# Tile 0's feed-forward products and pair 2's transposes: whole TensorE columns or halves of them

## The chip, the cores and the metric

The kernel runs on one core of one Trainium2 chip. The metric is the device time of one execution in microseconds; lower is better. TensorE (PE) does the matrix products, with its weight loads listed apart as PEld; VectorE (DVE), ScalarE (ACT), GpSimd (POOL) and SyncE (SP) do the rest. The DMA queues on POOL, SP and ACT carry the transfers.

## The reference

A retention layer is followed by a gated feed-forward layer. For 4 batches, 8 heads, 768 tokens and a head size of 64:

```
state = gamma[h] * state + k[t] (outer) v[t]      # for each batch and head
y[t]  = (1 / sqrt(64)) * q[t] @ state
x     = y as (3072 tokens, 512)
out   = (sigmoid(x @ w_gate) * (x @ w_val)) @ w_out     # w_gate, w_val: 512 x 1536; w_out: 1536 x 512
```

All inputs are float32; the kernel computes its products in bfloat16 and accumulates in float32.

## The kernel before

The 768 tokens of each batch are cut into 6 tiles of 128 tokens. A tile takes all 4 batches, so it is 512 rows of the feed-forward layer. The retention part of a tile is done in two *pairs* of batches: pair i belongs to tile i // 2 (pairs 0 and 1 to tile 0, pair 2 and 3 to tile 1, and so on).

For each pair, the keys and queries are needed with the head size on the partitions (`kqT`). Pairs 0 and 1 get this by transposes on TensorE (`first_transpose`), pair 2 by `transpose(2, j)`, which multiplies with an identity matrix, and the pairs from 3 on by DMA transposes (`xbar`, tile `kqX`). Then come the scores (`scores` for tile 0, `quarter_scores` later, L248), their masking on VectorE (`mask`), the part of y that comes from the state (`inter`, L271), the part within the tile (`intra`, L278), the copy of y into `xT` (`y_out`), and the state itself (`first_state` for tile 0, L378; `state`, L301).

For each tile, the feed-forward layer is done in 12 groups, one for each slice n1 of 128 hidden columns: a gate product and a value product over 4 slices kk of the model size, a sigmoid on ScalarE and a multiplication on VectorE into `hT`. Then `down` does the output products, four blocks b of 128 rows, each a sum over the 12 slices, with a copy on ScalarE and a store.

The schedule is written by hand: the order of the calls is the order of the instructions on each engine. A `plan` says after which feed-forward group a retention step of a later tile is inserted. PSUM has 8 banks in rotation (`bank`); an instruction that takes a bank waits until its last reader is done.

Tile 0 has an order of its own. Its first four hidden slices are computed by `first_parts` (L409), which takes the products as the weights and the columns of x arrive; slices 4 and 5 by `up_part`; then `first_state` for both pairs; then slices 6 to 11; then `down` for tile 0, with the transposes, scores, y and state of pair 2 between its parts.

How a product is issued is the matter of the change. `product(split, o, w, x)` issues either one matmul with 128 weight columns (which the profile lists as 128*128), or two with 64 weight columns each, whose results go to the lower and the upper 64 partitions (128*64). It is line L391 for both. In tiles 1 to 5 the products are in halves; in tile 0 they are whole, apart from the last six of block 3. `first_parts` calls the matmul itself, always whole. The two retention products `intra` and `state` are in halves anyway (a head has 64 columns), and `quarter_scores` and `inter` use quarters of the array (64*64).

`transpose` does whole transposes, for two heads at once: each takes 128 columns of k or q, and fills 128 partitions of the bank.

Of the kernel before, what the change touches and what calls it, by code (L numbers as in the profile page):

```python
# [15 lines left out]
def kernel(  # L16
# [12 lines left out]
    nc = tc.nc  # L29
    B, H, S, D = q.shape  # L30
    N_TOK, D_MODEL = out.shape
    D_FF = moe_w_gate.shape[1]
    C = 128
    NT = S // C
    NP = H // 2
    KT = D_MODEL // 128
    NFF = D_FF // 128
# [14 lines left out]
    def half(e):  # L52
        return slice(e * D, (e + 1) * D)
# [24 lines left out]
    wo = wpool.tile([128, NFF, D_MODEL], BF16, name="wo")  # L78
# [51 lines left out]
    ident = const.tile([128, 128], BF16, name="ident")  # L130
# [69 lines left out]
    def bank(shape, dt=F32):  # L200
        return pf.tile(shape, dt, tag="ff", name="ff")

    def heads(t, j, p):
        return t[:, j * H + 2 * p:j * H + 2 * p + 2, :].rearrange("s h d -> s (h d)")
# [4 lines left out]
    def transpose(i, j):  # L209
        tp = bank([128, 2, NP, C], BF16)  # L210
        for which, x in enumerate((kn[i], qn[i])):
            for p in range(NP):
                nc.tensor.transpose(tp[:, which, p, :], heads(x, j, p), ident)  # L213
        nc.scalar.copy(kqT[i][:, :, j], tp)

    def xbar(i):
# [68 lines left out]
    def x_of(t, kk, lo=0, hi=512):  # L285
        per = NP // len(xT[t])
        return xT[t][kk // per][:, kk % per, lo:hi]
# [20 lines left out]
    def state_sum(i):  # L308
        new_za(i)
        nc.vector.tensor_tensor(za[i], za[i - 2], zz[i], op=ALU.add)  # L310

    def casts(i):
        zb[i] = at.tile([128, 2, NP, D], BF16, tag="zb", name="zb", bufs=4)
        nc.vector.tensor_tensor(zb[i], za[i], tabz[:, i // 2 + 1].unsqueeze(3).to_broadcast([128, 2, NP, D]), op=ALU.mult)  # L314
# [69 lines left out]

    hT = {}

    def product(split, o, w, x, **marks):

        for g in range(2) if split else (None,):
            c = slice(0, 128) if g is None else half(g)  # L390
            nc.tensor.matmul(o[c], w[:, c], x, **marks)  # L391

    def up_part(t, w, n1s, lo=0, hi=512):
        n = hi - lo
        u = bank([128, 512])
        for i, n1 in enumerate(n1s):
            for kk in range(KT):
                product(t > 0, u[:, i * n:(i + 1) * n], w[:, kk, n1 * 128:(n1 + 1) * 128], x_of(t, kk, lo, hi),
                        start=(kk == 0), stop=(kk == KT - 1))
        return u[:, :len(n1s) * n]  # L400

    def first_parts(w, n1s, cut=512):

        us = [bank([128, 512]) for _ in range(2)]
        for k0, lo, hi in ((0, 0, cut), (0, cut, 512), (2, 0, 512)):
            for n1, u in zip(n1s, us):
                for kk in range(k0, k0 + 2):
                    if lo < hi:
                        nc.tensor.matmul(u[:, lo:hi], w[:, kk, n1 * 128:(n1 + 1) * 128], x_of(0, kk, lo, hi),  # L409
                                         start=(lo == 0 and kk == 0), stop=(kk == KT - 1), skip_group_check=True)  # L410
        return us

    def gate_times_val(t, n1s, lo, hi, ps):
# [9 lines left out]
    def up(t, n1s, lo=0, hi=512):  # L423
        gate_times_val(t, n1s, lo, hi, [up_part(t, w, n1s, lo, hi) for w in (wg, wv)])
# [3 lines left out]
    def rows(t, b):  # L428
        return b * S + t * C

    def down(t, b, lo, hi, split=None):
        split = t > 0 if split is None else split
        if lo == 0:
            po[b] = bank([128, 512])
        o = po[b]
        for n1 in range(lo, hi):
            product(split, o, hT[t][:, n1, b * C:(b + 1) * C], wo[:, n1, :], start=(n1 == 0), stop=(n1 == NFF - 1))
        if hi < NFF:
            return
        ob = ffn.tile([128, D_MODEL], F32, tag="ob", name="ob", bufs=4)  # L440
        nc.scalar.copy(ob, o)  # L441
        nc.sync.dma_start(out=out[rows(t, b):rows(t, b) + C, :], in_=ob)

    def last_down(t):
        row = rows(t, B - 1)
        lo = 0
        for i, width in enumerate((256, 128, 128)):
            o = bank([128, 512])
            for n1 in range(NFF):
                product(True, o[:, :width], hT[t][:, n1, 384:512], wo[:, n1, lo:lo + width],  # L450
                        start=(n1 == 0), stop=(n1 == NFF - 1))

            for g in range(1 + i // 2):
                n = width // (1 + i // 2)
                ob = ffn.tile([128, n], F32, tag=f"ob{i}{g}", name="ob", bufs=1)
                copy, eng = (nc.vector.tensor_copy, nc.sync) if i == 0 or g == 1 else (nc.scalar.copy, nc.scalar)
                copy(ob, o[:, g * n:(g + 1) * n])  # L457
                eng.dma_start(out=out[row:row + C, lo:lo + n], in_=ob)  # L458
                lo += n
# [47 lines left out]
    for n1s in ((0, 1), (2, 3)):  # L507
        gates = first_parts(wg, n1s, 3 * C if n1s[0] == 0 else 512)
        for n1, *ps in zip(n1s, gates, first_parts(wv, n1s)):
            gate_times_val(0, (n1,), 0, 512, ps)  # L510
    last_constants()
    zero_scores()
    later_tables()
    gates = [up_part(0, wg, (n1,)) for n1 in (4, 5)]
    for n1, gate in zip((4, 5), gates):
        gate_times_val(0, (n1,), 0, 512, (gate, up_part(0, wv, (n1,))))
# [23 lines left out]
    scale_k(2)  # L540
    new_kqT(2)
    down(0, 0, 0, 6)
    transpose(2, 0)
    down(0, 1, 0, 6)
    transpose(2, 1)
    down(0, 2, 0, 6)
    for b in range(3):
        down(0, b, 6, 9)
# [17 lines left out]
        y_out(2, j)  # L566
    state(2)
    state_sum(2)
    down(0, 3, 6, 12, True)
    casts(2)  # L570


# [12 lines left out]
    for t in range(1, NT):  # L585
        groups = [lambda n1=n1: up(t, (n1,)) for n1 in range(NFF)]
        if t == 1:
            groups = [lambda lo=lo, n1=n1: up(1, (n1, n1 + 1), lo, lo + 256) for lo in (0, 256) for n1 in range(0, NFF, 2)]
        groups += [lambda b=b, lo=lo: down(t, b, lo, lo + 6) for b in range(B) for lo in (0, 6)]
        if t == NT - 1:  # L590
            groups[-2:] = [lambda: last_down(t)]
        for i, group in enumerate(groups):
            group()
            for at_group, step, *g in plan[t]:
                if at_group == i:
                    step(*g)
# [30 lines left out]
```

## Time and profile before

| what | value |
|---|---|
| median of 4 runs | 224.52 us (223.89 to 225.24) |
| the profiled execution: time | 224.95 us |
| the profiled execution: span of the core | 223.2 us |
| granted TensorE clock, mean | 0.998 |
| TensorE busy (matmuls) | 216.3 us, 2760 instructions |
| TensorE busy (weight loads) | 126.4 us, 2760 instructions |
| VectorE, ScalarE, GpSimd busy | 124.8, 70.7, 100.3 us |

The profiled execution's time holds its span and 1.75 us around it. Matmuls overlap in the pipeline, so the time that one takes in a stream is read from the distance between starts and not from the mean duration of a group. A form such as 128*64 128x512 means 128 rows and 64 columns of weights, and 512 columns streamed.

### The profile page before, as it was taken

How to read it: one execution, taken by the hardware profiler on the slowest of the kernel's cores; microseconds unless marked ns; L12 is line 12 of the kernel's file. 1: busy time of each engine (PE TensorE's matmuls, PEld its weight loads, DVE VectorE, ACT ScalarE, POOL GpSimd, SP SyncE). 2: the span in 40 equal slices, each digit the busy share in tenths (PEclk: the TensorE clock that was granted, in tenths of full speed). 3: DMA queues.
4: the chain of work that ended last, by engine and by line, in shares of the span. 5: the costliest groups of instructions: out<-in, count | busy, mean ns of one | idle time of the engine just before them, and what ended most of it. 6: DMA issues, size and time to landing. Idle time of an engine off the chain costs nothing.

```text
span 223.2 us, 6371 instructions
## 1 busy us (share of the span) xinstructions
PE 216.3 (97%) x2760; PEld 126.4 (57%) x2760; DVE 124.8 (56%) x252; ACT 70.7 (32%) x123; POOL 100.3 (45%) x120
## 2 busy tenths in 40 slices
PE   7789999999999999999999999999999999999994
PEld 2543444559999565556556556555555555555554
DVE  6783983094984785656916645925644922333301
ACT  5883232334233213332222332321332322333221
POOL 7999646877796638709568091460000000000000
PEclk9999999999999999999999999999999999999999
DMA  9999999999999999989999999899600012100022
GB/s 132 139 161 183 197 203 172 174 131 248 162 127 148 151 163 146 169 96 62 131 126 184 165 64 106 80 137 140 141 3 0 3 47 97 47 4 1 3 94 94
DMA packets 105964, 25.84 MB, mean 116 GB/s; under 512 B 95056, under 2 KB 102992, under 8 KB 105936
## 3 DMA queue, kind: packets, MB, share of 16 engines
q0 software_dynamic: 80960, 13.90, 82.8%
q1 hardware_dynamic: 23648, 11.18, 24.1%
q10 hardware_dynamic: 1328, 0.36, 0.7%
q8 instruction: 21, 0.34, 0.6%
q14 instruction: 7, 0.06, 0.1%
HBM read 28.31 MB, written 6.29 MB: 155 GB/s over the span
## 4 chain that ended last, share of the span: by engine, by line
PE 90%; POOL 5%; DMA 2%; issue 0%; ACT 0%; ACTq 0%; DVE 0%; POOLq 0%
PE ff L391 81%; PE ff L278 3%; DMA wv<-in_moe_w_val_dram 2%; PE ff L409 2%; PE ff L248 2%; POOL vs L95 2%; PE ff L271 2%; POOL qn L95 1%; POOL kn L95 1%; PE ff L301 1%; POOL wg L82 1%; PE ff L213 0%; PE ff L378 0%; ACT ob L457 0%; ACTq L458 0%
## 5 line engine op out<-in xcount | busy, mean ns | idle before, releaser
L420 DVE TENSOR_TENSOR hT<-gs,ff 128x512 bf16<-128x512 f32 x72 | 48.4, 686 | 50.7 <-PE ff L391 46.8
L391 PE MATMUL ff<-xT,wg 128*64 128x512 bf16 (+2 forms) x608 | 70.1, 346 | 0.0
L391 PE MATMUL ff<-xT,wv 128*64 128x512 bf16 (+2 forms) x608 | 70.0, 345 | 0.0
L419 ACT ACTIVATE gs<-ff 128x512 f32<-128x512 f32 x72 | 42.8, 597 | 84.0 <-PE ff L391 78.6
L391 PE MATMUL ff<-wo,hT 128*64 128x512 bf16 (+3 forms) x582 | 64.7, 361 | 0.0
L391 PEld LDWEIGHTS <-wv 128*64 128x64 bf16 (+1 forms) x608 | 35.4, 109 | 23.5
L391 PEld LDWEIGHTS <-hT 128*64 128x64 bf16 (+1 forms) x582 | 32.7, 109 | 27.1
L391 PEld LDWEIGHTS <-wg 128*64 128x64 bf16 (+1 forms) x608 | 34.7, 109 | 23.1 <-DVE xT L294 0.6
L261 DVE TENSOR_TENSOR st<-ff,maskk 128x256 bf16<-128x256 f32 (+2 forms) x76 | 35.1, 493 | 7.4 <-PE ff L248 6.4
L441 ACT COPY ob<-ff 128x512 f32<-128x512 f32 x23 | 13.5, 586 | 56.5 <-PE ff L391 56.4
L294 DVE TENSOR_TENSOR xT<-ff,taby 128x512 bf16<-128x512 f32 x20 | 12.9, 686 | 23.5 <-PE ff L278 23.5
L224 POOL TENSOR_TENSOR ks<-kn,tabsk 128x1024 bf16<-128x1024 bf16 x8 | 15.4, 1929 | 2.4 <-DMA kn<-in_k_dram 2.2
L537 POOL COPY held<-kqX 128x1 bf16<-128x1 bf16 x7 | 1.3, 187 | 33.5 <-DMA kqX<-qn 31.0
L70 POOL DMA_DIRECT2D kn<-in_k_dram x20 | 15.1, 765 | 2.4 <-DMA kn<-in_k_dram 1.3
L70 POOL DMA_DIRECT2D qn<-in_q_dram x20 | 15.3, 790 | 0.8 <-DMA wv<-in_moe_w_val_dram 0.6
L60 POOL DMA_DIRECT2D vs<-in_v_dram x10 | 12.0, 1205 | 1.7 <-DMA wo<-in_moe_w_out_dram 1.0
L66 POOL DMA_DIRECT2D kn<-in_k_dram x10 | 9.2, 921 | 2.1 <-issue 1.5
L66 POOL DMA_DIRECT2D qn<-in_q_dram x10 | 9.1, 913 | 0.9 <-DMA wv<-in_moe_w_val_dram 0.9
L314 DVE TENSOR_TENSOR zb<-za,tabz 128x512 bf16<-128x512 f32 x10 | 7.3, 735 | 0.0
L464 PE MATMUL ff<-zero 128*128 128x512 bf16 x14 | 5.8, 543 | 1.2 <-DVE zero L139 1.2
L278 PE MATMUL ff<-st,vs 128*64 128x128 bf16 x160 | 6.4, 222 | 0.0
L82 POOL DMA_DIRECT2D wv<-in_moe_w_val_dram x8 | 6.2, 795 | 0.0
(74 smaller groups left out, 114.9 us busy)
## 6 DMA issues: line engine op xcount, KB each, us to landing
out_dram<-ob SPq DMA_DIRECT2D x23, 256.0 KB, 2.6
vs<-in_v_dram POOLq DMA_DIRECT2D x10, 256.0 KB, 7.2
kn<-in_k_dram POOLq DMA_DIRECT2D x13, 128.0 KB, 4.5
qn<-in_q_dram POOLq DMA_DIRECT2D x13, 128.0 KB, 4.8
wo<-in_moe_w_out_dram POOLq DMA_DIRECT2D x4, 384.0 KB, 9.6
kn<-in_k_dram POOLq DMA_DIRECT2D x20, 64.0 KB, 4.6
qn<-in_q_dram POOLq DMA_DIRECT2D x20, 64.0 KB, 4.8
wg<-in_moe_w_gate_dram POOLq DMA_DIRECT2D x4, 256.0 KB, 7.3
```

The source lines that it names most:

```text
L60: nc.gpsimd.dma_start(out=vs[i], in_=v[2 * h:2 * h + 2, :, t * C:(t + 1) * C, :].rearrange("b h s d -> s (b h) d"))
L66: nc.gpsimd.dma_start(out=tiles[i][:, 0:H], in_=src[0])
L70: nc.gpsimd.dma_start(out=dst[:, e], in_=pairs[:, 1 - e])
L95: eng.dma_start(out=dst, in_=x[b:b + n, :, 0:C, :].rearrange("b h s d -> s (b h) d"))
L224: nc.gpsimd.tensor_tensor(ks[i], kn[i], tabsk[:, i // 2].rearrange("s j h -> s (j h)").unsqueeze(2) .to_broadcast([C, 2 * H, D]), op=ALU.mult)
L261: nc.vector.tensor_tensor(st[i, j][to, :, n], sc[i, j][e][of, :, n], maskk[to, e ^ j, :, n], op=ALU.mult)
L278: nc.tensor.matmul(y[i, j][half(e), p, :], vs[i][:, j * H + 2 * p + e, :], st[:, p, :], start=False, stop=True, skip_group_check=True)
L294: nc.vector.tensor_tensor(xT[t][0][:, :, c:c + C], y[i, j], taby, op=ALU.mult)
L391: nc.tensor.matmul(o[c], w[:, c], x, **marks)
L419: nc.scalar.activation(g, ps[0], AX.Sigmoid)
L420: nc.vector.tensor_tensor(hT[t][:, n1s[0]:n1s[-1] + 1, lo:hi], g.rearrange("p (i n) -> p i n", n=n), ps[1].rearrange("p (i n) -> p i n", n ...
L441: nc.scalar.copy(ob, o)
```

## The change

Every product of tile 0 is issued as two halves, like the products of the other tiles: `product` loses its argument `split`, and `first_parts` uses it too. The 36 products of `first_parts`, 64 of `up_part` and 42 of `down` that were whole become two matmuls with two weight loads each. The 16 transposes of pair 2 become 32: each takes the 64 columns of one head and fills one half of the partitions. TensorE has 316 instructions more (158 matmuls and 158 weight loads). The order of the work, the banks and the other engines' instructions stay as they were.

```diff
         for which, x in enumerate((kn[i], qn[i])):
             for p in range(NP):
-                nc.tensor.transpose(tp[:, which, p, :], heads(x, j, p), ident)
+                for e in range(2):
+                    nc.tensor.transpose(tp[half(e), which, p, :], x[:, j * H + 2 * p + e, :], ident)
         nc.scalar.copy(kqT[i][:, :, j], tp)
...
-    def product(split, o, w, x, **marks):
-
-        for g in range(2) if split else (None,):
-            c = slice(0, 128) if g is None else half(g)
-            nc.tensor.matmul(o[c], w[:, c], x, **marks)
+    def product(o, w, x, **marks):
+
+        for g in range(2):
+            nc.tensor.matmul(o[half(g)], w[:, half(g)], x, **marks)
...
-                product(t > 0, u[:, i * n:(i + 1) * n], w[:, kk, n1 * 128:(n1 + 1) * 128], x_of(t, kk, lo, hi),
+                product(u[:, i * n:(i + 1) * n], w[:, kk, n1 * 128:(n1 + 1) * 128], x_of(t, kk, lo, hi),
                         start=(kk == 0), stop=(kk == KT - 1))
...
-                        nc.tensor.matmul(u[:, lo:hi], w[:, kk, n1 * 128:(n1 + 1) * 128], x_of(0, kk, lo, hi),
-                                         start=(lo == 0 and kk == 0), stop=(kk == KT - 1), skip_group_check=True)
+                        product(u[:, lo:hi], w[:, kk, n1 * 128:(n1 + 1) * 128], x_of(0, kk, lo, hi),
+                                start=(lo == 0 and kk == 0), stop=(kk == KT - 1), skip_group_check=True)
...
-    def down(t, b, lo, hi, split=None):
-        split = t > 0 if split is None else split
+    def down(t, b, lo, hi):
...
-            product(split, o, hT[t][:, n1, b * C:(b + 1) * C], wo[:, n1, :], start=(n1 == 0), stop=(n1 == NFF - 1))
+            product(o, hT[t][:, n1, b * C:(b + 1) * C], wo[:, n1, :], start=(n1 == 0), stop=(n1 == NFF - 1))
...
-    down(0, 3, 6, 12, True)
+    down(0, 3, 6, 12)
```

## The prediction

> **What bounds the kernel now.** I read the page first: the busy shares of the engines, then the chain of work that ended last.
>
> ```profile
> PE 216.3 (97%) x2760; PEld 126.4 (57%) x2760; DVE 124.8 (56%) x252; ACT 70.7 (32%) x123; POOL 100.3 (45%) x120
> PE 90%; POOL 5%; DMA 2%; issue 0%; ACT 0%; ACTq 0%; DVE 0%; POOLq 0%
> q8 instruction: 21, 0.34, 0.6%
> ```
>
> TensorE is busy for 97% of the span and is 90% of the chain. Next I listed the chain in order of time (start, length, what):
>
> ```profile
> 11.98 5.56 DMA wv<-in_moe_w_val_dram
> 17.54 0.05 issue
> 17.58 5.35 PE ff L409 x24
> 22.94 3.45 PE ff L391 x16
> 26.39 0.63 PE ff L378 x32
> 27.02 11.76 PE ff L391 x54
> ...
> 119.29 18.13 PE ff L391 x168
> ```
>
> Up to 17.58 us the chain is loads; from there to 219.5 us it is TensorE without a break. So a nanosecond saved on TensorE after 17.58 us is a nanosecond of the run, as long as nothing else takes over, and one saved before is lost in the wait for the first piece of w_val. The same rows give the price of a product. Undivided, 16 take 3.45 us: 216 ns each. In halves, 168 instructions are 84 pairs in 18.13 us: 216 ns a pair. Both run at a granted clock of 1.0. The division itself is thus worth nothing; what can differ is the place where TensorE goes from one form to another. For that I read TensorE's instructions in order of time around the first states of tile 0 (L378) and around an ordinary state in tile 2 (L301), which has halves on both sides:
>
> ```profile
> 24.50 1.89 PE L391 MATMUL ff<-xT,wv 128*128 128x512 bf16 x8
> 26.32 0.69 PE L378 MATMUL ff<-vs,ks 128*64 128x64 bf16 x32
> 26.95 1.04 PE L391 MATMUL ff<-xT,wg 128*128 128x512 bf16 x4
> 27.82 1.03 PE L391 MATMUL ff<-xT,wv 128*128 128x512 bf16 x4
> ```
>
> ```profile
> 98.58 1.03 PE L391 MATMUL ff<-xT,wv 128*64 128x512 bf16 x8
> 99.44 0.42 PE L301 MATMUL ff<-vs,ks 128*64 128x64 bf16 x16
> 99.69 1.03 PE L391 MATMUL ff<-xT,wg 128*64 128x512 bf16 x8
> 100.56 1.03 PE L391 MATMUL ff<-xT,wv 128*64 128x512 bf16 x8
> ```
>
> The lengths overlap because matmuls are pipelined, so only starts are compared. In tile 0, eight products from 24.50 us should let the next instruction start at 24.50 + 8 x 0.2158 = 26.23; the state starts at 26.32, 0.09 us late. In tile 2, 98.58 + 4 x 0.2158 = 99.44 is exactly where the state starts. The state's 16 instructions take 99.69 - 99.44 = 0.25 us there, so 32 would take 0.50; in tile 0 they take 26.95 - 26.32 = 0.63. After them the first four products take 0.87 us instead of 0.863. The columns before the shape explain it: 128*128 against 128*64. Going between them costs some 0.1 us each way.
>
> **The change part by part.**
>
> *Products of tile 0, from 17.58 us on.* There are 24 from the helper that begins with gates 0 to 3, 64 undivided ones from the gate and value groups after it, and 42 from the output products: 130, each replaced by two half instructions with two weight loads. At 216 ns for a pair as for one, the cost is 0. The 12 before 17.58 us lie ahead of the wait for w_val: there TensorE's last product starts at 16.69 us, so it has 0.68 us before it could be late.
>
> *The form changes around the first states.* Removed: 0.09 us before, 0.63 - 0.50 = 0.13 us in and behind, 0.01 us in the products after: 0.23 us, all on the path.
>
> *The form changes that stay.* The scores and the y of pair 2 use quarters of the array (64*64), which neither form shares:
>
> ```profile
> 38.61 0.39 PE L213 MATMUL ff<-ident,kn 128*128 128x128 bf16 x4
> ...
> 39.06 1.46 PE L391 MATMUL ff<-wo,hT 128*128 128x512 bf16 x6
> ...
> 40.80 3.40 PE L391 MATMUL ff<-wo,hT 128*128 128x512 bf16 x15
> 44.13 0.55 PE L248 MATMUL ff<-kqT 64*64 64x128 bf16 x32
> ...
> 48.30 0.64 PE L278 MATMUL ff<-st,vs 128*64 128x128 bf16 x16
> 48.77 0.42 PE L301 MATMUL ff<-vs,ks 128*64 128x64 bf16 x16
> ```
>
> From undivided products into the scores: 40.80 + 15 x 0.2158 = 44.04 against 44.13, 0.09 us. From halves into quarters, in tile 1, the trace has 18 pairs from 74.06 us and the next y at 78.04: 78.04 - 74.06 - 3.88 = 0.10 us. So these two entries keep their price, and the way out of the scores stays near 0.13 us for either. Small change: the second of two halves starts 3 to 4 ns after the first, twice 0.004 us; and the first products after a pause lose some 0.02 us as halves (56.13 to 57.03 us in tile 1: 0.90 for 8 pairs of 256 columns, where 0.873 is usual), against 0.01 undivided, at 17.58 and at 44.61 us: 0.02 us. Together +0.03 us.
>
> *The 16 transposes of pair 2 become 32.* Eight take 39.06 - 38.61 = 0.45 us. The nearest row of the new shape (128*64, 128 columns streamed, a new weight for each) is L278: 16 in 48.77 - 48.30 = 0.47 us, which holds the 0.02 us of a start after a form change. So between 0 and +0.04 us for both groups; I take 0, since these transposes now follow halves. A rule of the Trainium skill speaks against this part and is weighed here apart: the page "TensorEngine Tiling (Array Packing)", section "Gotcha 2: Feature Incompatibilities", says that column tiling excludes the fast weight load, and "TensorE: Matmul & The Clock Gate", section "LDWEIGHTS (loading the stationary operand)", gives columns / 1.2 in ns for a plain load. By the pages a half's load would be about 53 ns, an estimate, so 32 transposes would need 1.7 us instead of 0.9, and the whole change would come out at some +0.6 us. L278 disagrees: its instructions follow each other at 28 to 29 ns, each with its own load, so the measured row decides.
>
> *Who might be late next.* TensorE arrives up to 0.2 us earlier from 27 us on. The trace's landing times show the room: qn of pair 2 for its first transposes lands at 38.30 us and is used at 38.84 (0.54 us, the tightest); the third part of w_out lands at 41.07 and is used at about 42.1; the last at 42.99, used after 44.61. The banks of the groups are freed by ScalarE and VectorE over 2 us ahead (VectorE ends the product of n1 = 4 at 27.7 us; its bank is wanted at 30.4). In later tiles the closest DMA transpose lands at 83.4 us for the scores at 85.1. So nothing takes the 0.20 us back. No wait is added.
>
> Sum: -0.23 + 0.03 + 0 = -0.20 us. The profiled execution took 224.95 us with a span of 223.2, so one like it would take 224.75. The median of the runs is 224.52, 0.43 lower; from it, 224.3 us.
>
> **The rivals.**
>
> *Slower: instruction code in the way of a load.* The change adds 316 rows to TensorE's 5522. The trace has 21 fetches of 16 KB on the queue named instruction (0.34 MB over TensorE's 5522 rows is 62 bytes a row, so one holds some 260 rows), at 15.4, 32.4 and 48.2 us first, each 0.9 to 1.2 us long on one of the DMA engines. The one at 15.4 us shows the price: of the 16 landings of the first w_val piece, the fifteenth is at 16.72 and the last at 17.54 us, 0.82 later, where its neighbours show 0.2 to 0.4. So a fetch delays a load by about 0.55 us. With the halves the next ones would come at about 26 and 38 us. It decides if the fetch near 38 us begins before qn's landing at 38.30 and pushes it past 38.64, where the faster TensorE wants it: then 0.55 less the 0.34 of room, or more if the wait for w_val grows as well, up to 0.55. Net between 0 and +0.35 us: 224.5 to 224.9. Against it: the last landing of qn holds the lag left by the fetch at 32.4, which would now come at 26 us, where room is over 1 us.
>
> *Faster: the same fetch misses w_val.* If code is fetched so much earlier or later that it no longer delays the first w_val piece, TensorE starts up to 0.55 us sooner: 224.3 - 0.55 = 223.75. Against it: halves are consumed faster by at most some tenths of a microsecond between 15.15 and 15.4, and the engine that carries both has the same bytes to move before 17.54.
>
> *No gain.* The 0.1 us after the first states is not the form change but a wait that stays. Then some 0.1 us remains: 224.4. Against it: the same 0.09 to 0.13 us stands at each change of form, whatever the instruction waits for.
>
> *The halves do not overlap in tile 0.* Each of 130 products would cost up to 216 ns more, 28 us. Against it are 84 pairs at 216 ns. I keep it only as part of the chance below.
>
> **How the numbers follow.** The forecast of -0.1 to -0.3 us has 0.66; the slower rival 0.13; the faster one 0.09; no gain 0.06; anything else, mostly slower, 0.06. About 0.5% (1.1 us) is what a measurement of this kernel can tell from no change, and forecast, fetch and no-gain cases all lie within it: 0.88. Faster by more would need the missed fetch and more beside it: 0.05. Slower by more would need an unforeseen cost, or two delayed loads: 0.07. The range takes in both fetch rivals and the scatter of a median (the runs shown go from 223.89 to 225.24): 223.6 to 225.0.
>
> **What would show it.** Right: the state of tile 0 starts 8 pairs' time after its predecessors with no 0.09 us, its 32 instructions take 0.50 us, 16 transposes take 0.45 us, and everything from 49 us on stands 0.2 us earlier relative to the first w_val product. Wrong: transposes at 50 ns or more each; a pair of halves above 216 ns; a wait of TensorE for qn, w_gate or w_val after 17.6 us; or a first w_val product away from 17.58 us by more than 0.3.

## The result, and the profile after

The changed kernel takes 225.05 us (median of 44 runs, 224.19 to 226.29), the kernel before 224.57 us (median of 63 runs taken beside it, 223.89 to 225.76). The ratio is 1.0024, with a 95% interval from 1.0015 to 1.0032: 0.54 us slower, where 0.2 us less was forecast. The profiled execution took 225.51 us with a span of 223.7, against 224.95 and 223.2 before. Its mean granted clock is 0.991: the clock was at half from 8.2 to 11.6 us, ahead of the wait for w_val, and full from 11.6 us to the last product.

What the change was to do, it did. First the two places where TensorE changed its form, again as starts in order of time. The state of tile 0 (now L379), and the transposes (L214) up to the next output products:

```profile
24.69 1.89 PE L391 MATMUL ff<-xT,wv 128*64 128x512 bf16 x16
26.42 0.67 PE L379 MATMUL ff<-vs,ks 128*64 128x64 bf16 x32
26.92 1.03 PE L391 MATMUL ff<-xT,wg 128*64 128x512 bf16 x8
27.79 1.03 PE L391 MATMUL ff<-xT,wv 128*64 128x512 bf16 x8
...
38.58 0.39 PE L214 MATMUL ff<-ident,kn 128*64 128x128 bf16 x8
...
39.02 1.46 PE L391 MATMUL ff<-wo,hT 128*64 128x512 bf16 x12
```

Eight pairs of 0.2158 us from 24.69 end at 26.42, where the state starts: the 0.09 us are gone. The 32 instructions of the state take 0.50 us instead of 0.63. Eight half transposes of k and eight of q take 0.44 us together, four and four whole ones took 0.45. The chain in order of time begins differently, however:

```profile
12.43 6.15 DMA wv<-in_moe_w_val_dram
18.58 0.04 issue
18.62 7.96 PE ff L391 x72
26.58 0.50 PE ff L379 x32
```

It leaves the loads at 18.6 instead of 17.5 us. TensorE did start on the first w_val piece earlier than before, at 16.81 instead of 17.58 us, but then it waited for the second one:

```profile
16.81 1.03 PE L391 MATMUL ff<-xT,wv 128*64 128x512 bf16 x8
18.62 1.05 PE L391 MATMUL ff<-xT,wv 128*64 128x512 bf16 x8 [0.78 <-DMA wv<-in_moe_w_val_dram]
```

The products of the second piece start at 18.62; before, they started at 18.46. The first pair after the wait also takes 0.24 us instead of 0.216, so the eight products ahead of the state start at 24.69 us, where they started at 24.50. So 0.19 us were lost here and 0.21 won behind it: the y of pair 2 starts at 47.93 us (47.95 before), and the last matmul of the program at 219.91 us (219.92 before). Up to the end of TensorE's work the two profiles are level.

The 0.59 us by which the span is longer lie behind the start of TensorE's last matmul. The list of DMA issues has the four last stores; the last column is the time from issue to landing. Before:

```profile
out_dram<-ob SPq DMA_DIRECT2D x1, 128.0 KB, 1.7
out_dram<-ob ACTq DMA_DIRECT2D x1, 64.0 KB, 1.6
out_dram<-ob ACTq DMA_DIRECT2D x1, 32.0 KB, 1.5
out_dram<-ob SPq DMA_DIRECT2D x1, 32.0 KB, 1.5
```

After, with the line of the queue that carries instruction code:

```profile
q8 instruction: 23, 0.38, 0.7%
...
out_dram<-ob SPq DMA_DIRECT2D x1, 128.0 KB, 2.9
out_dram<-ob ACTq DMA_DIRECT2D x1, 64.0 KB, 2.5
out_dram<-ob ACTq DMA_DIRECT2D x1, 32.0 KB, 2.2
out_dram<-ob SPq DMA_DIRECT2D x1, 32.0 KB, 2.1
```

And from the order of time, the issues of the first and fourth of these stores (SPq, merged into one row, from the start of the first to the end of the fourth) and of the third (ACTq). Before:

```profile
219.30 1.74 SPq L458 DMA_DIRECT2D out_dram<-ob  x2
220.45 0.34 ACTq L458 DMA_DIRECT2D out_dram<-ob  x1
```

After:

```profile
219.28 2.08 SPq L457 DMA_DIRECT2D out_dram<-ob  x2
220.43 0.92 ACTq L457 DMA_DIRECT2D out_dram<-ob  x1
```

The trace's records show what is new there. TensorE's code comes in fetches of 16 KB, each a single packet, and this program has 23 of them where the kernel before has 21. The last one starts at 219.72 us, as TensorE runs its last products, and takes 1.24 us. A store is spread over 16 landings: of the first of the four, the fifteenth is at 221.00 and the last at 222.16 us (before: 220.99 and 221.01). One late landing of 16 fits a packet that keeps one DMA engine busy; the trace does not say which engine carried it. The issue of the third store takes 0.92 us and that of the fourth 0.68 instead of 0.33, so these two land late as a whole. From the start of the last matmul to the last landing it is 2.88 us, 2.25 before. In the kernel before the last fetch starts at 211.81 us, eight microseconds ahead of the end.

### The profile page after: what moved, and what is told of

It is laid out like the page before. It is cut to its first block, busy times and chain, and to the rows that moved or that the text cites. A ratio compares the mean times of both kernels' runs of the same rounds, so it can differ in the third digit from the quotient of the medians.

```text
span 223.7 us, 6685 instructions
## 1 busy us (share of the span) xinstructions
PE 216.4 (97%) x2918; PEld 128.6 (57%) x2918; DVE 125.8 (56%) x252; ACT 70.9 (32%) x123; POOL 100.0 (45%) x120
## 4 chain that ended last, share of the span: by engine, by line
PE 90%; POOL 5%; DMA 3%; issue 0%; DVE 0%; ACT 0%; POOLq 0%
PE ff L391 83%; DMA wv<-in_moe_w_val_dram 3%; PE ff L279 3%; PE ff L249 2%; POOL vs L95 2%; PE ff L272 2%; POOL kn L95 1%; POOL qn L95 1%; PE ff L302 1%; POOL wg L82 1%; PE ff L214 0%; POOL wv L82 0%; PE ff L379 0%; POOL ahead L112 0%; DVE ob L456 0%
## 5 line engine op out<-in xcount | busy, mean ns | idle before, releaser
L391 PE MATMUL ff<-xT,wv 128*64 128x512 bf16 (+1 forms) x672 | 74.0, 349 | 0.8 <-DMA wv<-in_moe_w_val_dram 0.8
L391 PE MATMUL ff<-xT,wg 128*64 128x512 bf16 (+3 forms) x680 | 73.9, 347 | 0.0
L391 PE MATMUL ff<-wo,hT 128*64 128x512 bf16 (+2 forms) x624 | 64.8, 363 | 0.0
L391 PEld LDWEIGHTS <-wv 128*64 128x64 bf16 x672 | 37.6, 110 | 25.7 <-DMA wv<-in_moe_w_val_dram 1.3
L391 PEld LDWEIGHTS <-wg 128*64 128x64 bf16 x680 | 37.2, 110 | 24.0 <-DVE xT L295 0.6
L391 PEld LDWEIGHTS <-hT 128*64 128x64 bf16 x624 | 33.4, 110 | 26.5
L440 ACT COPY ob<-ff 128x512 f32<-128x512 f32 x23 | 13.5, 586 | 56.5 <-PE ff L391 56.4
```

The costliest lines, as they stand in the source:

```text
L391: nc.tensor.matmul(o[half(g)], w[:, half(g)], x, **marks)
```

## The experiments

The theory (E) was that the loss is this last fetch, which depends on the number of TensorE's instructions and not on what tile 0 does with them. The rivals were that the halves of the products (P) or of the transposes (T) cost it. All numbers of instructions below are TensorE's; the kernel before has 5522, the changed one 5838, and a fetch of 16 KB holds 256 if a row takes 64 bytes. Every version ran beside the kernel before: e1 to e4 on one chip, e5 to e8 on another and f1 to f4 on a third, where the kernel before had medians of 224.50, 224.62 and 224.56 us. So between versions of different groups the ratios compare better than the medians.

This table gathers the end of all profiles, from the trace's records of the code queue and of the landings. The tail is the time from the start of the last matmul to the last landing.

| version | instructions | last fetch starts, from the start of the last matmul | tail, us | median, us | ratio to before, with interval |
|---|---|---|---|---|---|
| before | 5522 | -8.1 us | 2.25 | 224.57 | |
| after | 5838 | -0.2 | 2.88 | 225.05 | 1.0024 (1.0015 to 1.0032) |
| e1, products only | 5806 | -10.6 | 2.24 | 224.74 | 1.0013 (0.9995 to 1.0032) |
| e2, transposes only | 5554 | +5.0, one more at -10.9 | 2.24 | 225.22 | 1.0032 (1.0014 to 1.0050) |
| e3, before + 96 | 5618 | -1.0 | 2.39 | 225.55 | 1.0044 (1.0023 to 1.0065) |
| e4, after + 128 | 5966 | -5.3 | 2.24 | 224.42 | 0.9995 (0.9981 to 1.0009) |
| e5, before + 320 | 5842 | -0.1 | 2.67 | 226.55 | 1.0084 (1.0053 to 1.0114) |
| e6, after + 256 | 6094 | +0.1 | 2.70 | 226.11 | 1.0064 (1.0041 to 1.0088) |
| e7, after + 126 early | 5964 | -5.2 | 2.24 | 226.14 | 1.0064 (1.0037 to 1.0091) |
| e8, before + 126 early | 5648 | -2.2 | 2.23 | 225.90 | 1.0041 (1.0018 to 1.0063) |
| f1, before + 64 spread | 5586 | +0.1 | 3.13 | 225.24 | 1.0039 (1.0020 to 1.0059) |
| f2, after + 64 spread | 5902 | -1.7 | 2.24 | 224.43 | 0.9989 (0.9972 to 1.0007) |
| f3, after + 256 spread | 6094 | -0.1 | 2.97 | 225.03 | 1.0025 (1.0008 to 1.0041) |
| f4, after, first slices whole | 5766 | -8.2 | 2.24 | 224.82 | 1.0020 (0.9994 to 1.0045) |

**e1: the halves of the products alone.** The changed kernel with the transposes as before:

```diff
-                for e in range(2):
-                    nc.tensor.transpose(tp[half(e), which, p, :], x[:, j * H + 2 * p + e, :], ident)
+                nc.tensor.transpose(tp[:, which, p, :], heads(x, j, p), ident)
```

> The products of tile 0 in halves, the 16 transposes whole: 5806 instructions on TensorE instead of 5838. Theory E (the loss is one more fetch of instruction code, which falls on the last stores because of the number of instructions): the program ends 32 instructions before the point that set off the fetch at 219.7 us, so the page shows 22 fetches or fewer with none after 218 us, the last store lands as before (about 1.7 us after its issue), and the 0.2 us of removed form changes show: 0.1 to 0.3 us below the kernel before. Rival T (the transposes in halves cost what is lost): also faster than after, but with a fetch at the end. Rival P (the halves of the products cost it): 0.4 to 0.6 us above the kernel before, as after.

The late fetch is gone and the tail is 2.24 us, as theory E had it. But the time is 0.3 us above the kernel before by the ratio (interval 0.1 below to 0.7 above), not below it; by its time alone e1 does not rule out rival P. The expectation had forgotten what the prediction had counted elsewhere: whole transposes between halves bring four changes of form. From the first state (25.89) to the y of pair 2 (47.86) it is 21.97 us, where the changed kernel has 21.51. So in this profile the 0.2 us turn into a loss of as much when the transposes do not change with the products.

**e2: the halves of the transposes alone.** The kernel before, with the two lines of the change in `transpose`.

> The kernel before with the 16 transposes of pair 2 as 32 halves and nothing else: 5554 instructions. Theory E: no fetch at the end, and four changes of form more around the transposes (about 0.1 us each): 0.2 to 0.5 us above the kernel before. Rival T: 0.5 us or more, with the transposes themselves above 0.45 us for 16. Rival P: as theory E.

Again four changes of form: from the state (26.23) to the y of pair 2 (48.31) it is 22.08 us against 21.63 before, 0.45 us. Within a group, two half transposes take 56 ns, as one whole transpose does, so the transposes themselves cost nothing, against rival T. The median is 0.7 us above the kernel before. Its trace has a fetch of code that starts 1.8 us after the span has ended, and the profiled execution took 2.84 us more than its span. But the other eight runs took 1.72 to 1.92 more, and the median span is 223.5 us against 222.75 of the kernel before. So the loss lies within the span, and where the other 0.3 us of it come from is not shown.

**e3 and e4: only the number of instructions.** In tile 3, products of 512 columns are done as two runs of 256, which is the same arithmetic: 24 products in the kernel before, and 32 in the changed kernel (shown; in the kernel before `product` has its argument as well, and n1 = 6 is left out).

```diff
-            for kk in range(KT):
-                product(u[:, i * n:(i + 1) * n], w[:, kk, n1 * 128:(n1 + 1) * 128], x_of(t, kk, lo, hi),
-                        start=(kk == 0), stop=(kk == KT - 1))
+            cut = 2 if t == 3 and n1 in (3, 4, 5, 6) else 1
+            for c in range(cut):
+                a, b = lo + c * n // cut, lo + (c + 1) * n // cut
+                for kk in range(KT):
+                    product(u[:, i * n + a - lo:i * n + b - lo], w[:, kk, n1 * 128:(n1 + 1) * 128], x_of(t, kk, a, b),
+                            start=(kk == 0), stop=(kk == KT - 1))
```

> The kernel before, with 24 products of tile 3 cut into two runs of 256 columns each: the same arithmetic, 96 instructions more on TensorE (5618), none of them in tile 0. Theory E: one more fetch comes in the last 4 us and delays the last landings by about 0.6 us; the cut costs 24 x 2.7 ns = 0.06 us; together +0.5 to +0.7 us. Rivals T and P: +0.06 us only.

> The changed kernel with 32 products of tile 3 cut in the same way: 128 instructions more (5966). Theory E: the fetch that fell on the last stores comes about 128 instructions, some 2 us, earlier and is over before they are issued; the cut costs 0.09 us: 0 to 0.2 us below the kernel before, that is faster than after although it does more. Rivals T and P: 0.09 us above after, some 0.6 us above the kernel before.

Both came out on the side of theory E: e3 is 1.0 us slower than the kernel before, although tile 0 is untouched, and e4, with more instructions and more work than the changed kernel, is 0.63 us faster than it by the medians and level with the kernel before. But the tail of e3 is only 0.14 us longer in its profile. That execution, at 224.93 us, was the third lowest of twelve; where the rest of the 1.0 us comes from is not shown.

**e5 and e6: larger counts.** The same cut for 80 products of the kernel before, and for 64 of the changed one.

> The kernel before, with 80 products of tile 3 cut into two runs of columns: tile 0 as before, but 5841 instructions, four more than the changed kernel. Theory E (one more fetch of code falls on the last stores, by the number of instructions alone): 0.22 us for the cut and 0.6 to 1.0 us for the fetch: +0.8 to +1.2 us, with a fetch after 218.5 us in the profile. Rival (the loss comes from what tile 0 does): +0.22 us, no late landings.

> The changed kernel with 64 products of tile 3 cut: 6093 instructions, a whole fetch (256) more than the changed kernel, 128 more than the version that lost the late fetch. Theory E: the late fetch is back in the last microseconds, so the time goes up by 0.6 us and 0.09 us for the cut against that version, to some 225.2 (0.5 to 0.9 us above the kernel before). Rival (more instructions move the time evenly, or the gain of that version was chance): within 0.2 us of that version.

The late fetch is in both profiles, with tails of 2.67 and 2.70 us, and both are slower than the rivals allow. But they are slower than theory E allows too: 1.9 us for e5, and 1.7 us above e4 for e6. The profile of e6 shows another loss. In order of time, TensorE in tile 3, with the idle time ahead of an instruction in brackets:

```profile
139.02 1.04 PE L391 MATMUL ff<-xT,wv 128*64 128x256 bf16 x16
139.90 0.38 PE L391 MATMUL ff<-xT,wg 128*64 128x512 bf16 x2
140.89 0.84 PE L391 MATMUL ff<-xT,wg 128*64 128x512 bf16 x6 [0.61 <-issue]
```

In the last row it waits for nothing that the profile shows (`issue`). The trace has a fetch of code from 138.09 to 139.44 us: 74 instructions ran between its start and the stop, and the next ones ran 1.45 us after its end. The cut products use up four instructions in 0.11 us instead of 0.22. The likely reading is that TensorE had run out of code, so that the pads, lying close together, brought a loss of their own. The profiles of e3 and e5 have no such stop, but they are of executions well below the medians (e5's 225.46 us is the lowest of its six runs), so for these two the reading is only argued. All three say less of the last fetch than they were meant to.

**e7 and e8: the first fetch.** The first 9 matmuls on zeros become 72 of 64 columns each, so that the code of tile 0 moves by 126 instructions:

```diff
-    def keep_on(n):
+    def keep_on(n, cut=1):
         u = bank([128, 512])
-        for _ in range(n):
-            nc.tensor.matmul(u, zero[:, :128], zero, start=True, stop=True)
+        for _ in range(n * cut):
+            nc.tensor.matmul(u[:, :512 // cut], zero[:, :128], zero[:, :512 // cut], start=True, stop=True)
...
-    keep_on(9)
+    keep_on(9, 8)
```

> The changed kernel, whose first 9 matmuls on zeros (512 columns) are 72 of 64 columns: the same time for them, 126 instructions more, but at the start, so that the total (5963) is that of the version with 128 late ones, and the first fetch of code comes some 126 instructions sooner, near 9 to 12 us instead of 15 to 16.5. Theory F (the first fetch also decides when the first w_val pieces land): both pieces land with at most 0.4 us between the fifteenth and the last of their 16 landings, TensorE works through from about 16.8 us, and the time is 0.1 to 0.6 us below the version with 128 late ones. Rival: the pieces land as before the pad, and the time is at most 0.1 us below it (the cut that is not paid).

> The kernel before with the same 72 short matmuls at the start: 5647 instructions; tile 0 whole. Theory F: the first w_val piece is no longer held up, TensorE starts on it at 16.7 to 17.0 us instead of 17.4 to 17.6, and the time is 0.4 to 0.7 us below the kernel before. With theory E no fetch comes after 219 us (the last one starts about 130 instructions before the end). The difference to the changed kernel with the same start is then the form changes alone, 0.2 us. Rival: no change, within 0.1 us of the kernel before.

Both failed. In e7 the first fetch did move, to 9.54 us, and the first two w_val pieces land with 0.0 and 0.1 us between the fifteenth and the last landing; the products of the second piece start at 17.94 us. But the later fetches moved as well, and one now came ahead of the state of pair 4:

```profile
73.35 0.32 PE L302 MATMUL ff<-vs,ks 128*64 128x64 bf16 x8
74.54 0.32 PE L302 MATMUL ff<-vs,ks 128*64 128x64 bf16 x8 [0.87 <-issue]
```

115 instructions ran between the start of that fetch (71.77 us) and the stop, and TensorE stood for 1.0 us in the midst of the 16 of the state. In e8 the granted clock of the profile was 0.54 from 13.5 to 16.9 us, and the first products came at 17.16 instead of 15.15 us, too late to show what the first fetch does. None of its twelve runs is below 224.66 us, so the gain that theory F forecast is seen in none. What the first fetch is worth is not settled.

**f1, f2, f3: the pads spread.** To take the dense cuts out of the test, only single products are cut: kk = 1 of some gate products in tiles 2 to 5, so that no two cuts follow each other (shown for f2; f1 does the same to the kernel before, and f3 takes all twelve slices of w_gate and 1, 4, 7 and 10 of w_val).

```diff
             for kk in range(KT):
-                product(u[:, i * n:(i + 1) * n], w[:, kk, n1 * 128:(n1 + 1) * 128], x_of(t, kk, lo, hi),
-                        start=(kk == 0), stop=(kk == KT - 1))
+                cut = 2 if kk == 1 and t > 1 and n1 in ((2, 5, 8, 11) if w is wg else ()) else 1
+                for c in range(cut):
+                    a, b = c * n // cut, (c + 1) * n // cut
+                    product(u[:, i * n + a:i * n + b], w[:, kk, n1 * 128:(n1 + 1) * 128], x_of(t, kk, lo + a, lo + b),
+                            start=(kk == 0), stop=(kk == KT - 1))
```

> The kernel before, with one product of four w_gate groups in each of tiles 2 to 5 cut into two runs of 256 columns: 16 cuts, spread so that nowhere two lie together, 64 instructions more (5586: 252 fewer than the changed kernel, which is 4 short of one fetch of 256). Tile 0 is untouched. Theory E (an additional fetch on the last stores): +0.04 us for the cuts and +0.4 to +0.8 us, with a fetch after 218 us and a last landing over 0.4 us later than before, seen from the last product. Rival (what was lost before is tile 0's, and the dense cuts of the earlier padded versions had starved TensorE of code): +0.04 us.

> The changed kernel with the same 16 cuts, 5902 instructions. Theory E: the late fetch comes some 64 instructions earlier or falls behind the stores; 0.3 to 0.7 us below the changed kernel, which is 224.3 to 224.8 us, from 0.3 us below the kernel before to 0.2 above it. Rival: 0.04 us above the changed kernel, about 225.1 us.

> The changed kernel with 64 such cuts spread over tiles 2 to 5: 6094 instructions, exactly one fetch more than the changed kernel. Theory E, which goes by the place of the last fetch and not by their number: as the changed kernel and 0.17 us for the cuts, 225.0 to 225.5 us, that is slower than the version with 64 cuts by 0.5 us or more. Rival (each instruction more costs something): between the changed kernel and 0.2 us above it as well, but then the version with 64 cuts is not below the changed kernel.

All three came out as theory E had them. With 64 instructions more, the kernel before loses 0.7 us (medians, 225.24 against 224.56) and the changed kernel gains 0.6; with 192 more, f3 is back at 225.03. The interval of f2's ratio lies below those of f1 and f3. No stop of TensorE without a wait stands in the three profiles, as it does in e6; but f3's (226.02 us, the longest of its twelve runs) has a wait of 0.68 us for w_gate at 23.18 us, so for f3 the medians are compared and not this execution's time. The last two stores in f1 (the kernel before, whole tile 0, and a fetch at 219.80 us for 1.25 us), by the list of issues:

```profile
out_dram<-ob ACTq DMA_DIRECT2D x1, 32.0 KB, 2.6
out_dram<-ob SPq DMA_DIRECT2D x1, 32.0 KB, 2.2
```

and in f2 (the changed kernel, with its last fetch from 217.59 to 218.64 us):

```profile
out_dram<-ob ACTq DMA_DIRECT2D x1, 32.0 KB, 1.5
out_dram<-ob SPq DMA_DIRECT2D x1, 32.0 KB, 1.5
```

So the late landings go with the place of the last fetch, in either kernel, and not with halves. In the table the tail is long (2.67 to 3.13 us) in the five profiles whose last fetch before the end starts within 0.2 us of the last matmul, 2.39 where it starts 1.0 us ahead, and 2.23 to 2.25 wherever it starts 1.7 us ahead or more. The counts say the same. Divided by 256, the five programs with a long tail leave a remainder of 206 to 210, e3 leaves 242, and the others 14 to 178. In this order of the remainders the last fetch before the end lies further and further ahead of the last matmul, up to 10.9 us (134 and 146 alone are level). f2 has the lowest ratio of all versions, 0.9989, but its interval reaches 1.0007: it is not shown to beat the kernel before.

**f4: the first slices whole.** The changed kernel with the matmul of `first_parts` as before.

> The changed kernel with the 36 products of the first four slices whole again (5766 instructions); the rest of tile 0 and the transposes in halves. No fetch at the end by theory E. The form changes around the first states are gone, one of 0.09 us is added where the halves begin at 22.8 us: 0.1 us less than the kernel before. The first fetch of code meets the first w_val piece as in the kernel before, so TensorE starts on it at 17.4 to 17.6 us and goes on without a second wait. Together 224.3 to 224.6 us. If the second wait for w_val that the changed kernel shows is a part of its loss, this version is below the changed kernel with 64 cuts; if not, level with it.

The median of 224.82 us lies above what was expected, and the runs scatter from 224.01 to 227.22. The interval holds both a gain of 0.1 us and a loss of 1.0. Its profile (224.01 us) also shows a wait between the two pieces of w_val, with the second piece's products at 17.64 us; so do those of f1 and e5, where tile 0 is that of the kernel before (18.23 and 18.32). So the second wait is not a mark of the halves. On the time, this run decides nothing.

## Why the prediction was wrong

**Right: the products are level.** A pair of halves takes 0.2158 us in tile 0 as elsewhere.

**Right: the form changes.** From the eight products ahead of the first states to the y of pair 2, 0.21 us were won, where the sum had 0.20, and the transposes cost nothing more; by the estimate that the prediction drew from the Trainium skill and set aside (53 ns for each half's load) they would have taken 1.7 us, and they took 0.9.

**Wrong: "nothing takes the 0.20 us back".** This is the step that failed. It went through the loads that TensorE waits for, the banks and the DMA transposes, and stopped at TensorE's last product: what comes behind it stood at nothing, without a reason. The last stores have no work beside them and count in full; with the additional fetch the time from the last matmul's start to the last landing grew by 0.63 us. The sum for the profile is -0.21 (forms) + 0.19 (second piece of w_val) + 0.63 (last stores) - 0.02 (behind the last landing) = 0.59 us, which is the difference of the spans. f1 and f2 show the loss of the stores to go with the place of the fetch. That the 0.2 us of the forms reach the time of the whole is not shown: without the late fetch, e4 and f2 are at 0.9995 and 0.9989, with intervals that hold 1.

**Half right: the rival with instruction code.** Its mechanism fits: beside a fetch of 16 KB the last landing of a transfer comes late, by more than the 0.55 us that it was given (1.16 us behind the fifteenth, for the first of the last stores). Its place was wrong. It was put at the loads of pair 2 and at w_val, and the fetches were counted on from the first ones only. Counted back from the end, the trace before has 242 matmuls and weight loads behind the start of its last fetch, at 211.81 us. With 316 more there are 558, room for one more fetch with 302 left and another, 256 later, with 46 left, close to the last stores; the trace after has them at 322 and 14. The rival had 0.13, and its range ended at 224.9.

**The first w_val products.** They were to stay within 0.3 us of 17.58 and started at 16.81. That sign tells nothing of the halves: with the first products whole they start at 16.89 in f1 and at 17.40 in e3. The condition of the faster rival was met in this execution: the first fetch starts at 16.50 instead of 15.41 us, behind the last landing of the first piece (16.34). But the second piece then has its fifteenth landing at 16.94 and its last at 18.58 us (before: 17.44 and 17.88), so the early start ended in a wait. That the fetch did this is not shown; in e1, with a fetch at 15.69, the same distance is 1.1 us. What counts is the second piece's products: 18.46 us before, 18.62 after. Over the profiles of all versions, e8 aside, they start between 17.63 and 18.62 with halves and between 17.64 and 18.46 with whole first products. One profile of each cannot tell these apart; the 0.19 us are this execution's, and how the front differs in the mean stays open.

The Trainium skill describes these fetches, and the prediction did not draw on it there: "Runtime: NRT & Kernel Launch", section "Instruction fetch mechanics", says that code is refilled in blocks of 16 KiB, 256 instructions, over a queue of the sequencer's own, while the current block runs. The 16 KB packets agree. The page calls the cost of a block's boundary mostly hidden. The runs agree for most of them; but not for the one that meets the last stores (0.6 to 0.7 us on the median, f2 and f1), nor, as the profiles of e6 and e7 are read above, for one that meets dense code (0.6 and 0.9 us of idle TensorE).

## What to carry to other kernels

A change that adds instructions to a full engine also moves the fetches of the code that follows. Count the instructions back from the end of the program: if the last fetch falls on the last stores, which nothing hides, some dozens of instructions more or fewer can be worth more than the change itself, here 0.6 to 0.7 us for 64. And when a change of a few tenths of a microsecond is judged, compare it with a version of the same instruction count (here, the same remainder by 256), with pads that are spread out.

## What was not expected of the hardware

- A fetch of code that starts within 0.2 us of the last matmul went with a longer time from that matmul to the last landing, 2.67 to 3.13 us in five profiles instead of about 2.24. One landing of 16 is late, and the issue of the third of the last stores takes 0.67 to 1.16 us instead of 0.34.
- TensorE seems to have run out of code in two profiles. In e6 and e7 it stood still until 2.8 us after the start of a fetch, having done 74 and 115 instructions in less time than that: dense products of 256 columns, and the short products of scores and states.
- The time is not even in the number of instructions: the changed kernel with 0, 64, 128 and 256 more takes 225.05, 224.43, 224.42 and 225.03 us (the 128 lie close together, the others are spread).
